# First chunk of a SiLU MLP kernel: eight groups on 384 transposed rows over narrow w1 slices, then on the last 128 rows in the same banks

## The chip, the cores and the metric

The kernel runs on one core of one Trainium2 chip. The metric is the device time of one execution in microseconds (us). Each run is marked as fast or slow (slow when over 1.5% above the fastest of its kernel); medians are over all runs of a set and given with the lowest and highest run.

PE is TensorE (matmuls), PEld its weight loads, ACT is ScalarE, DVE is VectorE, SP is SyncE. PE, ACT, DVE and SP each have a queue of instructions; DMAs are issued from SP and ACT here. "Landing" is the time at which all sixteen DMA engines have reported their share of a DMA. PSUM is the memory in which matmuls add up their results; the kernel uses eight banks of it, each of 128 x 512 fp32. A start flag marks the matmul that begins a new sum in a bank. The "grant" is the moment from which PE runs at its full clock. The chain that ended last is the row of waits and work that the profile follows back from the last instruction.

## The reference

A SiLU MLP, forward and backward, in bfloat16, with S = 2048 rows, D = 640, F = 1536:

```python
h   = x @ w1            # (S, F)
a   = silu(h)
out = a @ w2            # (S, D)
# and the gradients of x, w1, w2 for a given grad_out
```

The four outputs are `out`, `gx`, `gw1` and `gw2`.

## The kernel before

The rows are worked off in four chunks of 512. For a chunk, twelve groups (F = 12 x 128) of five matmuls (D = 5 x 128) make h transposed; ScalarE makes silu and tanh of it, VectorE the gradient factor. Then come `out` (the w2 phase) and the other gradients. From the w2 phase of the first chunk on, all operands are there in time, and PE works without a pause. The change is about what comes before: at the start nothing has been loaded, x must be transposed, and the first matmuls follow the DMAs.

The first chunk before: 256 rows of x are loaded and transposed on PE, the other 256 come through a DMA transpose, which landed 8.0 us after its issue. All twelve groups run first on the 256 PE-transposed rows, w1 slice by w1 slice (two groups share one PSUM bank), so that PE can start when the first of five slices is there (even its first half: slice 0 comes in two halves, one on each queue). Then all run on the other 256 rows.

```python
early += [load_x(nc.sync, 0), load_x(nc.scalar, 1)]
early += [load_w1(0, slice(0, F // 2)), load_w1(0, slice(F // 2, F), nc.scalar)]
early += [load_w1(k) for k in range(1, 3)]
for k in range(3, DT):
    load_w1(k)                                  # five slices of 128 x 1536, 393 KB each
nc.sync.dma_start_transpose(out=xT_next[:, :, HC:SC], in_=x2[HC:SC, :])     # HC = 256
...
def h_first(xT, aT, ghT):
    pe_x(xT)                                    # 10 transposes on PE, 3 copies
    halves = (slice(0, HC), slice(HC, SC))
    hs = [[ps_h.tile([P, 2, HC], FP32, name="hp") for _ in range(NPAIR)], []]
    for dt_ in range(DT):
        for pair in range(NPAIR):
            h_pair_mm(hs[0][pair], pair, dt_, xT, halves[0])        # 60 matmuls of 256 columns
    ...                                         # silu, four copies out of PSUM
    for pair in range(NPAIR):
        ...
        for q in range(2):
            for dt_ in range(DT):
                h_pair_mm(hp, pair, dt_, xT, halves[1], (q,))       # 60 more
        ...
```

Eighteen unneeded matmuls (`NWARM = 18`) run from the very start, before x is there, to bring PE to its fast clock.

Of the kernel before, what the change touches and what calls it, by code (L numbers as in the profile page):

```python
# [9 lines left out]
ACT = mybir.ActivationFunctionType  # L10
ALU = mybir.AluOpType
FP32 = mybir.dt.float32
# [3 lines left out]
def start_before_entry_wait(nc, names):  # L16




    def move(nc):
        blocks = nc.m.functions[0].blocks
        entry, home = blocks[0].instructions, blocks[1].instructions
        for engine in {i.engine for i in home if i.name in names}:
            mine = [i for i in home if i.engine == engine]
            last = max(k for k, i in enumerate(mine) if i.name in names)
            moved = mine[: last + 1]
            gate = next(
                k
                for k, i in enumerate(entry)  # L30
                if i.engine == engine and isinstance(i, mybir.InstEventSemaphore)
            )
            taken = {i.name for i in moved}
            for k in reversed(range(len(home))):
                if home[k].name in taken:
                    del home[k]
            for i in reversed(moved):
                entry.insert(gate, i)

    nc.at_finalize(move)  # L40
# [35 lines left out]
def kernel(  # L76
# [11 lines left out]
    nc = tc.nc  # L88
    P = 128
# [7 lines left out]
    F = w1.shape[1]  # L97
    ST, DT, FT = S // P, D // P, F // P
    SC = 512
# [4 lines left out]
    FB = FC // P  # L104
    LAG = 2
    NWARM = 18
    HC = 2 * P
    NPAIR = FT // 2
    NCOPY = 4
    dt_in = x.dtype  # L110

# [34 lines left out]
    with ExitStack() as mctx:  # L146
# [35 lines left out]
        def load_x(eng, q):  # L182
            return eng.dma_start(out=x_nat[:, q, :], in_=x_v[:, q, :])  # L183

        def load_w1(k, cols=slice(0, F), eng=nc.sync):
            return eng.dma_start(out=w1_nat[:, k, cols], in_=w1_v[:, k, cols])  # L186

        early += [load_x(nc.sync, 0), load_x(nc.scalar, 1)]
        early += [load_w1(0, slice(0, F // 2)), load_w1(0, slice(F // 2, F), nc.scalar)]
        early += [load_w1(k) for k in range(1, 3)]  # L190
        for k in range(3, DT):
            load_w1(k)
        nc.sync.dma_start_transpose(out=xT_next[:, :, HC:SC], in_=x2[HC:SC, :])
        start_before_entry_wait(nc, {i.ins.name for i in early})
        nc.scalar.activation(warm_a[:], warm[:, 0:1], ACT.Silu)
        nc.sync.dma_start(out=w2_nat[:], in_=w2_v[:])
# [4 lines left out]

        def pe_x(xT):
            slices = ((0, 1), (1, 3), (3, DT))
            tps = [ps_h.tile([P, hi - lo, 2, P], dt_in, name="tp", tag="hp") for lo, hi in slices]
            for q in range(2):
                for tp, (lo, hi) in zip(tps, slices):
                    for dt_ in range(lo, hi):
                        nc.tensor.transpose(
                            tp[:, dt_ - lo, q, :], x_nat[:, q, dt_ * P:(dt_ + 1) * P], ident[:]
                        )  # L210
            for k, (tp, (lo, hi)) in enumerate(zip(tps, slices)):
                copy_tp = nc.scalar.copy if k % 2 else nc.vector.tensor_copy
                copy_tp(out=xT[:, lo:hi, 0:HC], in_=tp[:].rearrange("p k q s -> p k (q s)"))

# [10 lines left out]
        def silu_a(ft, hp, aT):  # L225
            nc.scalar.activation(aT[:, ft, :], hp[:], ACT.Silu)  # L226
# [13 lines left out]
            silu_a(ft, hp, aT)  # L240
            silu_grad(ft, hp, aT, ghT)

        def h_pair_mm(hp, pair, dt_, xT, cols, qs=(0, 1)):
            for q in qs:
                ft = 2 * pair + q
                nc.tensor.matmul(  # L246
                    hp[:, q, :],
                    lhsT=w1_nat[:, dt_, ft * P:(ft + 1) * P],
                    rhs=xT[:, dt_, cols],
                    start=(dt_ == 0 and q == qs[0]),  # L250
                    stop=(dt_ == DT - 1 and q == qs[-1]),
                )

        def pair_silu(hp, pair, aT, cols):
            nc.scalar.activation(aT[:, 2 * pair:2 * pair + 2, cols], hp[:], ACT.Silu)

        def pair_grad(hp, pair, aT, ghT, cols):
            fts = slice(2 * pair, 2 * pair + 2)
            t = tpool.tile([P, 2, HC], FP32, name="t")
            nc.scalar.activation(t[:], hp[:], ACT.Tanh, scale=0.5)  # L260
            v = tpool.tile([P, 2, HC], dt_in, name="v")
            nc.vector.tensor_scalar(out=v[:], in0=t[:], scalar1=-0.5, scalar2=0.5, op0=ALU.mult, op1=ALU.add)
            nc.vector.scalar_tensor_tensor(
                out=ghT[:, fts, cols], in0=aT[:, fts, cols], scalar=1.0, in1=v[:],
                op0=ALU.subtract, op1=ALU.mult,
            )

        def h_first(xT, aT, ghT):
            pe_x(xT)
            halves = (slice(0, HC), slice(HC, SC))  # L270
            hs = [[ps_h.tile([P, 2, HC], FP32, name="hp") for _ in range(NPAIR)], []]
            for dt_ in range(DT):
                for pair in range(NPAIR):
                    h_pair_mm(hs[0][pair], pair, dt_, xT, halves[0])
            for pair in range(NPAIR):
                pair_silu(hs[0][pair], pair, aT, halves[0])
                if pair < NCOPY:
                    h_sb = hpool.tile([P, 2, HC], FP32, name="h_sb")
                    nc.vector.tensor_copy(out=h_sb[:], in_=hs[0][pair][:])
                    hs[0][pair] = h_sb  # L280
            grads = [(0, pair) for pair in list(range(NCOPY, NPAIR)) + list(range(NCOPY))]
            grads += [(1, pair) for pair in range(NPAIR)]
            for pair in range(NPAIR):
                hp = ps_h.tile([P, 2, HC], FP32, name="hp")
                hs[1].append(hp)
                for q in range(2):
                    for dt_ in range(DT):
                        h_pair_mm(hp, pair, dt_, xT, halves[1], (q,))
                pair_silu(hp, pair, aT, halves[1])
                if 1 <= pair <= 3:  # L290
                    half, done = grads.pop(0)
                    pair_grad(hs[half][done], done, aT, ghT, halves[half])
            for half, pair in grads:
                pair_grad(hs[half][pair], pair, aT, ghT, halves[half])

        def g_group(ft, goT, ghT):
            gp = ps_h.tile([P, SC], FP32, name="hp")
# [32 lines left out]
        for c in range(NCH):  # L330
            xT, goT = xT_next, goT_next
            aT = apool.tile([P, FT, SC], dt_in, name="aT")
            ghT = apool.tile([P, FT, SC], dt_in, name="ghT")

            if c + 1 < NCH:
                xT_next = load_xT(c + 1)
                goT_next = load_goT(c + 1)
            if c == 1:
                for j in range(0, ST, STC):
                    nc.sync.dma_start(out=go_nat[:, j:j + STC, :], in_=go_v[:, j:j + STC, :])  # L340
            if c == 2:
                for j in range(0, ST, STC):
                    rows = slice(max(j, 2), j + STC)
                    nc.sync.dma_start(out=x_nat[:, rows, :], in_=x_v[:, rows, :])

            if c == 0:
                h_first(xT, aT, ghT)
                nc.sync.dma_start(
                    out=aT_scr[:, c * SC:(c + 1) * SC].rearrange("(ft p) s -> p ft s", p=P), in_=aT[:]
                )  # L350
                sd_phase(c, w2_nat, aT, oT_scr)
                for ft in range(FT):
                    g_group(ft, goT, ghT)
                nc.sync.dma_start(
                    out=ghT_scr[:, c * SC:(c + 1) * SC].rearrange("(ft p) s -> p ft s", p=P), in_=ghT[:]
                )
                sd_phase(c, w1T, ghT, gxT_scr)
                continue

            for i in range(FT + LAG):  # L360
                if i < FT:
                    h_group(i, xT, aT, ghT)
                if i >= LAG:
                    g_group(i - LAG, goT, ghT)

            store_rows(c - 1, opool)
            nc.sync.dma_start(
                out=aT_scr[:, c * SC:(c + 1) * SC].rearrange("(ft p) s -> p ft s", p=P), in_=aT[:]
            )
            nc.sync.dma_start(  # L370
                out=ghT_scr[:, c * SC:(c + 1) * SC].rearrange("(ft p) s -> p ft s", p=P), in_=ghT[:]
            )
            if c == NCH - 1:
                load_a_blk(0, w1pool, "w1a")

            sd_phase(c, w2_nat, aT, oT_scr)
            sd_phase(c, w1T, ghT, gxT_scr)
# [121 lines left out]
```

## Time and profile before

| | before |
|---|---|
| time, first set | 320.62 us median of 3 (320.48 to 320.81) |
| span of the profiled execution | 318.8 us |
| PE busy | 313.6 us (98%) |
| PE's share of the chain that ended last | 96% |
| first w1 matmul / start of the w2 phase | 3.85 / 18.41 us |

The page's first part, busy time of each engine with its share of the span:

```profile
PE 313.6 (98%) x1516; PEld 150.5 (47%) x1544; DVE 102.8 (32%) x182; ACT 76.8 (24%) x139; POOL 0.7 (0%) x6
```

PE leaves almost nothing to win, except at the start. This is the chain that ended last, in order of time (start in us, duration in us, what):

```profile
1.47 6.41 DMA w_nat<-in_w_dram
7.88 0.05 issue
7.92 10.65 PE hp L246 x96
18.58 0.21 PE hp L315
```

The chain runs through a w1 slice until 7.88 us, then through 96 matmuls (L246) without a pause, then into the w2 phase (L315). The timeline of PE up to there has the start in us, the duration in us, engine, line, operation, shapes and count, and in brackets the idle time before, with what ended it:

```profile
0.50 2.10 PE L160 MATMUL wp<-warm 128*128 128x128 bf16 x18 [0.50 <-DVE warm L156]
2.64 1.25 PE L208 MATMUL tp<-ident,x_nat 128*128 128x128 bf16 x10
3.85 1.72 PE L246 MATMUL hp<-xT,w_nat 128*128 128x256 bf16 x12
5.79 1.48 PE L246 MATMUL hp<-xT,w_nat 128*128 128x256 bf16 x12 [0.22 <-DMA w_nat<-in_w_dram]
7.92 10.65 PE L246 MATMUL hp<-xT,w_nat 128*128 128x256 bf16 x96 [0.65 <-DMA w_nat<-in_w_dram]
18.41 13.11 PE L315 MATMUL hp<-aT,w_nat 128*128 128x512 bf16 x58
```

PE had to wait before its second and third row of twelve w1 matmuls. A bracket counts the wait from the modelled end of the matmul before; the starts of neighbouring matmuls are 0.38 and 0.82 us further apart than the usual 109 ns there, 1.20 us in all. The first row itself was a little slow: three of the spacings of its matmuls were 165 to 213 ns, 0.25 us too much.

### The profile page before, as it was taken

What the parts mean: (1) busy time and instruction counts of PE and PEld (TensorE: products, weight loads), DVE (VectorE), ACT (ScalarE), POOL (GpSimd) and SP (SyncE); (2) the same over time, 40 slices, a digit from 0 to 9 for tenths busy, and PEclk for the clock granted to TensorE, in tenths of its full rate; (3) what the DMA queues carried; (4) which work ended last, traced back from release to release, by engine and by line L of the source; (5) the groups of instructions that cost most, each with busy time, mean ns of one, the idle gap of its engine ahead of it and who ended that gap; (6) DMA issues with size and microseconds to landing.
All of it is one profiled execution on the core that took longest, in us unless ns stands there. A gap on an engine that the chain in (4) does not pass through costs nothing.

```text
span 318.8 us, 3632 instructions
## 1 busy us (share of the span) xinstructions
PE 313.6 (98%) x1516; PEld 150.5 (47%) x1544; DVE 102.8 (32%) x182; ACT 76.8 (24%) x139; POOL 0.7 (0%) x6
## 2 busy tenths in 40 slices
PE   8999999999999999999999999999999999999997
PEld 6854444444444444444444444444444444444444
DVE  1495641477410087710147741000000100001001
ACT  2691000545201354411054520110100001001010
POOL 0000000000000000000000000000000000000000
DMA  8999999999989986492635079909999999997111
GB/s 280 293 181 192 221 249 260 349 252 280 292 214 343 230 155 176 169 310 76 168 110 141 0 256 267 221 20 297 211 245 254 204 251 326 236 313 217 65 35 49
DMA packets 147233, 67.02 MB, mean 210 GB/s; under 512 B 113937, under 2 KB 146705, under 8 KB 147217
## 3 DMA queue, kind: packets, MB, share of 16 engines
q1 hardware_dynamic: 146928, 66.43, 83.3%
q10 hardware_dynamic: 288, 0.36, 0.3%
q8 instruction: 12, 0.20, 0.2%
q14 instruction: 5, 0.03, 0.0%
HBM read 9.18 MB, written 28.97 MB: 120 GB/s over the span
## 4 chain that ended last, share of the span: by engine, by line
PE 96%; DMA 2%; issue 1%; SPq 0%; DVE 0%; DVEq 0%
PE hp L315 32%; PE hp L299 16%; PE hp L404 16%; PE hp L455 15%; PE hp L217 12%; PE hp L246 3%; DMA w_nat<-in_w_dram 2%; PE hp L435 1%; SPq L186 0%; SPq L183 0%; DVE g L446 0%; DVEq L446 0%; SPq L483 0%
## 5 line engine op out<-in xcount | busy, mean ns | idle before, releaser
L299 PE MATMUL hp<-goT,w2T 128*128 128x512 bf16 x239 | 56.8, 379 | 0.1
L315 PE MATMUL hp<-ghT,w1T 128*128 128x512 bf16 x235 | 52.2, 379 | 0.3
L315 PE MATMUL hp<-aT,w_nat 128*128 128x512 bf16 x234 | 52.1, 379 | 0.3
L404 PE MATMUL hp<-a_blk,go_nat 128*128 128x512 bf16 x235 | 51.7, 379 | 0.3
L455 PE MATMUL hp<-gh_blk,x_nat 128*128 128x512 bf16 x219 | 48.2, 379 | 0.3
L217 PE MATMUL hp<-xT,w_nat 128*128 128x512 bf16 x174 | 43.4, 379 | 0.3
L323 ACT ACTIVATE oT<-hp 128x512 bf16<-128x512 f32 x24 | 14.5, 604 | 106.8 <-PE hp L315 106.8
L299 PEld LDWEIGHTS <-w2T 128*128 128x128 bf16 x240 | 23.5, 98 | 28.3
L404 PEld LDWEIGHTS <-go_nat 128*128 128x128 bf16 x240 | 23.5, 98 | 28.3
L315 PEld LDWEIGHTS <-w1T 128*128 128x128 bf16 x240 | 23.4, 98 | 28.4
L315 PEld LDWEIGHTS <-w_nat 128*128 128x128 bf16 x240 | 23.5, 98 | 28.1
L306 DVE SCALAR_TENSOR_TENSOR ghT<-ghT,hp 128x512 bf16<-128x512 bf16 x48 | 32.5, 683 | 7.3 <-PE hp L299 7.3
L455 PEld LDWEIGHTS <-x_nat 128*128 128x128 bf16 x224 | 21.9, 98 | 26.4
L325 DVE CAST oT<-hp 128x512 bf16<-128x512 f32 x16 | 11.1, 691 | 72.2 <-PE hp L315 67.7
L226 ACT ACTIVATE aT<-hp 128x512 bf16<-128x512 f32 x36 | 21.5, 597 | 30.4 <-PE hp L217 30.4
L217 PEld LDWEIGHTS <-w_nat 128*128 128x128 bf16 x180 | 17.6, 98 | 21.2
L233 DVE SCALAR_TENSOR_TENSOR ghT<-aT,v 128x512 bf16<-128x512 bf16 x36 | 24.7, 686 | 0.2
L232 DVE TENSOR_SCALAR v<-t 128x512 bf16<-128x512 f32 x36 | 15.4, 427 | 26.7 <-ACT t L230 26.7
L230 ACT ACTIVATE t<-hp 128x512 f32<-128x512 f32 x36 | 21.3, 591 | 0.0
L466 DVE CAST g<-hp 128x512 bf16<-128x512 f32 x7 | 4.8, 692 | 47.0 <-PE hp L455 27.0
L414 DVE CAST g2T<-hp 128x512 bf16<-128x512 f32 x7 | 4.8, 692 | 46.1 <-PE hp L404 46.1
L412 ACT ACTIVATE g2T<-hp 128x512 bf16<-128x512 f32 x8 | 4.8, 597 | 47.0 <-PE hp L404 47.0
(28 smaller groups left out, 76.4 us busy)
## 6 DMA issues: line engine op xcount, KB each, us to landing
aT_scr<-aT SPq DMA_DIRECT2D x4, 1536.0 KB, 6.3
ghT_scr<-ghT SPq DMA_DIRECT2D x4, 1536.0 KB, 8.2
out_dram<-o_sb SPq DMA_DIRECT2D x8, 640.0 KB, 3.3
oT_scr<-oT SPq DMA_DIRECT2D x4, 640.0 KB, 3.6
go_nat<-in_grad_out_dram SPq DMA_DIRECT2D x4, 640.0 KB, 8.1
gxT_scr<-oT SPq DMA_DIRECT2D x4, 640.0 KB, 4.8
w_nat<-in_w_dram SPq DMA_DIRECT2D x1, 1920.0 KB, 11.0
x_nat<-in_x_dram SPq DMA_DIRECT2D x3, 640.0 KB, 7.4
```

Source lines behind the costliest of these rows:

```text
L217: nc.tensor.matmul(hp[:], lhsT=w1_nat[:, dt_, ft * P:(ft + 1) * P], rhs=xT[:, dt_, :], start=(dt_ == 0), stop=(dt_ == DT - 1),)
L226: nc.scalar.activation(aT[:, ft, :], hp[:], ACT.Silu)
L230: nc.scalar.activation(t[:], hp[:], ACT.Tanh, scale=0.5)
L232: nc.vector.tensor_scalar(out=v[:], in0=t[:], scalar1=-0.5, scalar2=0.5, op0=ALU.mult, op1=ALU.add)
L233: nc.vector.scalar_tensor_tensor(out=ghT[:, ft, :], in0=aT[:, ft, :], scalar=1.0, in1=v[:], op0=ALU.subtract, op1=ALU.mult)
L299: nc.tensor.matmul(gp[:], lhsT=w2T[:, dt_, ft * P:(ft + 1) * P], rhs=goT[:, dt_, :], start=(dt_ == 0), stop=(dt_ == DT - 1),)
L306: nc.vector.scalar_tensor_tensor(out=ghT[:, ft, :], in0=ghT[:, ft, :], scalar=1.0, in1=gp[:], op0=ALU.add, op1=ALU.mult)
L315: nc.tensor.matmul(op_[:], lhsT=w_all[:, ft, dt_ * P:(dt_ + 1) * P], rhs=rhs_all[:, ft, :], start=(ft == 0), stop=(ft == FT - 1),)
L323: nc.scalar.activation(oT[:, dt_, :], op_[:], ACT.Copy)
L325: nc.vector.tensor_copy(out=oT[:, dt_, :], in_=op_[:])
L404: nc.tensor.matmul(gp[:], lhsT=go_nat[:, st, dt_ * P:(dt_ + 1) * P], rhs=a_blk[:, st, :], start=(st == 0), stop=(st == ST - 1),)
L455: nc.tensor.matmul(gp[:], lhsT=x_nat[:, st, dt_ * P:(dt_ + 1) * P], rhs=gh_blk[:, st, :], start=(st == 0), stop=(st == ST - 1),)
```

## The change

Its intent: the first part shall need fewer bytes of w1. Eight groups, one per bank, run on 384 PE-transposed rows over slices of 1024 columns (262 KB). The DMA transpose brings only 128 rows. When they are there, the same eight groups take them into the same banks (128 more columns of the bank, without a start flag), and the last four groups run on all 512 rows at once, with the last 512 columns of w1.

```diff
-    HC = 2 * P
-    NPAIR = FT // 2
+    NQ = 3
+    HC = NQ * P
+    NA = 8
+    FA = NA * P
...
-        early += [load_x(nc.sync, 0), load_x(nc.scalar, 1)]
-        early += [load_w1(0, slice(0, F // 2)), load_w1(0, slice(F // 2, F), nc.scalar)]
-        early += [load_w1(k) for k in range(1, 3)]
+        early += [load_x(nc.sync, 0), load_x(nc.scalar, 1), load_x(nc.sync, 2)]
+        early += [load_w1(0, slice(0, FA), nc.scalar)]
+        early += [load_w1(k, slice(0, FA)) for k in range(1, 3)]
         for k in range(3, DT):
-            load_w1(k)
+            load_w1(k, slice(0, FA))
         nc.sync.dma_start_transpose(out=xT_next[:, :, HC:SC], in_=x2[HC:SC, :])
+        nc.sync.dma_start(out=w1_nat[:, :, FA:F], in_=w1_v[:, :, FA:F])
...
-            for q in range(2):
+            for q in range(NQ):
...
+            for dt_ in range(DT):
+                for ft in range(NA):
+                    mm(ft, dt_, slice(0, HC), dt_ == 0, False)
+            for ft in range(NA):
+                for dt_ in range(DT):
+                    mm(ft, dt_, slice(HC, SC), False, dt_ == DT - 1)
+                silu_a(ft, hs[ft], aT)
+                if ft < NCOPY:
+                    h_sb = hpool.tile([P, SC], FP32, name="h_sb")
+                    nc.vector.tensor_copy(out=h_sb[:], in_=hs[ft][:])
+                    hs[ft] = h_sb
+            grads = list(range(NCOPY, NA))
+            for ft in range(NA, FT):
+                hs.append(ps_h.tile([P, SC], FP32, name="hp"))
+                h_mm(hs[ft], ft, xT)
+                silu_grad(grads[0], hs[grads[0]], aT, ghT)
+                grads.pop(0)
+                silu_a(ft, hs[ft], aT)
+            for ft in list(range(NA, FT)) + list(range(NCOPY)):
+                silu_grad(ft, hs[ft], aT, ghT)
```

More of the change, by code (lines that the diff above doesn't have):

```diff
@@ L203, in pe_x @@
             slices = ((0, 1), (1, 3), (3, DT))
-            tps = [ps_h.tile([P, hi - lo, 2, P], dt_in, name="tp", tag="hp") for lo, hi in slices]
-            for q in range(2):
+            tps = [ps_h.tile([P, hi - lo, NQ, P], dt_in, name="tp", tag="hp") for lo, hi in slices]
+            for q in range(NQ):
                 for tp, (lo, hi) in zip(tps, slices):
@@ L241, in h_group, with h_first, mm @@
             silu_grad(ft, hp, aT, ghT)
-        def h_pair_mm(hp, pair, dt_, xT, cols, qs=(0, 1)):
-            for q in qs:
-                ft = 2 * pair + q
+        def h_first(xT, aT, ghT):
+            pe_x(xT)
+            hs = [ps_h.tile([P, SC], FP32, name="hp") for _ in range(NA)]
+            def mm(ft, dt_, cols, start, stop):
                 nc.tensor.matmul(
-                    hp[:, q, :],
+                    hs[ft][:, cols],
                     lhsT=w1_nat[:, dt_, ft * P:(ft + 1) * P],
@@ L249, in h_pair_mm @@
                     rhs=xT[:, dt_, cols],
-                    start=(dt_ == 0 and q == qs[0]),
-                    stop=(dt_ == DT - 1 and q == qs[-1]),
-                )
-        def pair_silu(hp, pair, aT, cols):
-            nc.scalar.activation(aT[:, 2 * pair:2 * pair + 2, cols], hp[:], ACT.Silu)
-        def pair_grad(hp, pair, aT, ghT, cols):
-            fts = slice(2 * pair, 2 * pair + 2)
-            t = tpool.tile([P, 2, HC], FP32, name="t")
-            nc.scalar.activation(t[:], hp[:], ACT.Tanh, scale=0.5)
-            v = tpool.tile([P, 2, HC], dt_in, name="v")
-            nc.vector.tensor_scalar(out=v[:], in0=t[:], scalar1=-0.5, scalar2=0.5, op0=ALU.mult, op1=ALU.add)
-            nc.vector.scalar_tensor_tensor(
-                out=ghT[:, fts, cols], in0=aT[:, fts, cols], scalar=1.0, in1=v[:],
-                op0=ALU.subtract, op1=ALU.mult,
-            )
@@ L268, in h_first @@
-        def h_first(xT, aT, ghT):
-            pe_x(xT)
-            halves = (slice(0, HC), slice(HC, SC))
-            hs = [[ps_h.tile([P, 2, HC], FP32, name="hp") for _ in range(NPAIR)], []]
-            for dt_ in range(DT):
-                for pair in range(NPAIR):
-                    h_pair_mm(hs[0][pair], pair, dt_, xT, halves[0])
-            for pair in range(NPAIR):
-                pair_silu(hs[0][pair], pair, aT, halves[0])
-                if pair < NCOPY:
-                    h_sb = hpool.tile([P, 2, HC], FP32, name="h_sb")
-                    nc.vector.tensor_copy(out=h_sb[:], in_=hs[0][pair][:])
-                    hs[0][pair] = h_sb
-            grads = [(0, pair) for pair in list(range(NCOPY, NPAIR)) + list(range(NCOPY))]
-            grads += [(1, pair) for pair in range(NPAIR)]
-            for pair in range(NPAIR):
-                hp = ps_h.tile([P, 2, HC], FP32, name="hp")
-                hs[1].append(hp)
-                for q in range(2):
-                    for dt_ in range(DT):
-                        h_pair_mm(hp, pair, dt_, xT, halves[1], (q,))
-                pair_silu(hp, pair, aT, halves[1])
-                if 1 <= pair <= 3:
-                    half, done = grads.pop(0)
-                    pair_grad(hs[half][done], done, aT, ghT, halves[half])
-            for half, pair in grads:
-                pair_grad(hs[half][pair], pair, aT, ghT, halves[half])
@@ new lines, in mm @@
+                    start=start,
+                    stop=stop,
+                )
+            for dt_ in range(DT):
+                for ft in range(NA):
[8 more added lines that the diff above has]
+                    hs[ft] = h_sb
@@ L342 @@
                 for j in range(0, ST, STC):
-                    rows = slice(max(j, 2), j + STC)
+                    rows = slice(max(j, NQ), j + STC)
                     nc.sync.dma_start(out=x_nat[:, rows, :], in_=x_v[:, rows, :])
```

## The prediction

> **What bounds the kernel now.** TensorE (PE): busy 313.6 of 318.8 us (98%), 96% of the chain of waits that ended last. The change touches only the first 18 us, so it can win only what PE loses there. In the timeline the x transposes start at 2.64 us, the first w1 matmul (128x256) at 3.85, and PE stands before w1 slices until 5.79 (0.22 us idle) and 7.92 (0.65 us); the chain runs through that w1 load (1.47 to 7.88 us). From 7.92 the remaining 96 matmuls run unbroken at 109 ns each to 18.41, where the w2 phase begins. 3.85 plus 120 x 109 ns would be 16.9: about 1.5 us are lost, 0.25 to slow first matmuls (12 at about 131 ns), 1.2 to late w1.
>
> **What the change does, costed.**
> - Matmul time hardly changes. Spacings read from the trace: 512 columns 216 ns (five in 1.08 us), 256 columns 109; the kernel's last group (16 of 384 and 16 of 128 columns, 3.66 us) gives 162 and about 55. Before 120 x 109 = 13.1 us; after 40 x 162 + 40 x 55 + 20 x 216 = 13.0. The Trainium skill ("TensorE: Matmul & The Clock Gate", Back-to-back issue gap) has about 81 ns for 128 columns with weight loads; this trace decides, else +1 us.
> - Five more transposes (ten took 1.25 us) on a third x slice, and copies of 384 columns: the first w1 matmul moves from 3.85 to about 4.4 (+0.5).
> - x and w1 bytes before the first part can finish: 2.29 MB before, 1.80 after. PE still needs 1.3 us per w1 slice, but a slice is 262 KB, not 393. From arrivals before (4.1, 5.75, 7.88, about 8.7 and 9.8) I estimate 4.4, 5.3, 6.9, 7.9, 8.8. Then no slice costs PE more than about 0.2 us; the first part ends near 11.0, the twelve groups near 17.5 to 17.7.
> - New limit: w2 landed at 17.9 (issued 6.94, 11.0 to landing), 0.5 us before its use. The bytes ahead of it are the same; I expect 17.5 to 17.8, so it may take part back.
> - ScalarE/VectorE: eight silus from about 11.5 at about 0.5 us pitch, then alternating with four tanh; the last silu ends near 19.4, before its use at about 20.4. The gradient chain on VectorE ends about 1 us later (28), before its first use at 31.5. Banks come free in time.
> - One start flag per bank, then a second column range without it, is sound by the Trainium skill ("PSUM — Partial Sum Buffer", The four PSUM rules: the flag clears the whole bank's written bits).
>
> **On the critical path:** +0.5 (later start), -1.0 to -1.2 (w1 waits), -0.1 (matmul sum, slow matmuls), 0 to +0.2 (w2): net about -0.7 us. The other 300 us are untouched. Predicted 319.9 us, 8-in-10 range 319.3 to 320.9. Chances: faster by over 2% 0.01, within 2% 0.98, slower 0.01.
>
> **What would show it.** First w1 matmul at about 4.4; PE idle before w1 under 0.3 us; 128-column matmuls spaced 55 ns; the w2 phase at about 17.7, perhaps with idle put down to the w2 load; no new PE wait after; PE busy about the same.
>
> **What would make it wrong.** Slices arriving no earlier, because a slow DMA engine rather than bytes sets their landing (320.7 to 321.1); w2 late; 128-column matmuls at 80 ns; more slow matmuls; waits moved by the changed order of DMA semaphores.

## The result, and the profile after

| | before | after |
|---|---|---|
| time, median of 6 | 320.52 us (320.27 to 320.81) | 319.88 us (319.59 to 320.81) |
| ratio of fast runs | | 0.9984, 95% interval 0.9969 to 0.9999 |
| profiled execution | 320.54 us, span 318.8 | 320.81 us, span 319.0 |

A ratio is the mean time of one kernel's fast runs over that of the other's of the same rounds, so it isn't quite the ratio of the medians. The median fell by 0.64 us, to within 0.02 us of the prediction. But the execution that was profiled is the slowest of the six, slower than the one profiled before. The number came out right; the profile says something else than the prediction's sum.

The page's first part, after:

```profile
PE 314.5 (99%) x1501; PEld 147.7 (46%) x1529; DVE 102.9 (32%) x182; ACT 77.2 (24%) x139; POOL 0.7 (0%) x6
```

The chain that ended last, in order of time, after:

```profile
0.54 3.51 DMA x_nat<-in_x_dram
4.05 0.05 issue
4.10 0.71 PE tp L211 x5
4.81 0.02 issue
4.83 9.71 PE hp L251 x80
14.54 0.21 PE hp L220
...
18.86 6.69 PE hp L299 x31
```

The w1 load is gone from the chain. In its place stands the third x slice, which landed at 4.05 us, and from 4.83 us on nothing but PE. The timeline of PE, after (same columns as before):

```profile
0.51 2.10 PE L162 MATMUL wp<-warm 128*128 128x128 bf16 x18 [0.51 <-DVE warm L158]
2.56 1.25 PE L211 MATMUL tp<-ident,x_nat 128*128 128x128 bf16 x10
4.10 0.71 PE L211 MATMUL tp<-ident,x_nat 128*128 128x128 bf16 x5 [0.29 <-DMA x_nat<-in_x_dram]
4.83 9.71 PE L251 MATMUL hp<-xT,w_nat 128*128 128x384 bf16 x80
14.38 4.48 PE L220 MATMUL hp<-xT,w_nat 128*128 128x512 bf16 x19
18.70 13.11 PE L299 MATMUL hp<-aT,w_nat 128*128 128x512 bf16 x59
```

PE starts on w1 at 4.83 instead of 3.85 us and then has no pause; the w2 phase starts at 18.70 instead of 18.41. Where did the gain go? The timeline of the weight loads, which come one per matmul, shows it (after):

```profile
5.10 0.15 PEld L251 LDWEIGHTS <-w_nat 128*128 128x128 bf16 x1 [0.17 <-issue]
5.42 0.15 PEld L251 LDWEIGHTS <-w_nat 128*128 128x128 bf16 x1 [0.17 <-issue]
5.74 0.15 PEld L251 LDWEIGHTS <-w_nat 128*128 128x128 bf16 x1 [0.17 <-issue]
6.06 0.15 PEld L251 LDWEIGHTS <-w_nat 128*128 128x128 bf16 x1 [0.17 <-issue]
6.38 7.98 PEld L251 LDWEIGHTS <-w_nat 128*128 128x128 bf16 x74 [0.17 <-issue]
```

Until 6.4 us the loads, and so the matmuls of 384 columns, are 320 ns apart, then 162: PE ran on half its clock. The trace has a record of the full clock's being granted at 6.53 us after the first instruction. (The profile's column for the granted clock shows 1.00 from the start: it knows of no clock before its first record. One has to read the spacing.) The Trainium skill ("TensorE: Matmul & The Clock Gate", Part 1) describes this: PE's clock is halved until PE has been busy through a window of about 3.4 us, and these windows run freely, so that where the kernel's start falls in one is chance. In the execution profiled before, the full speed came at about 4.4 us.

From this, four numbers make up the start of the w2 phase: the first w1 matmul; the matmuls at full speed (13.1 us before, and 40 x 162.5 + 40 x 56 + 20 x 216 ns = 13.06 us after); half of the time spent at half the clock; and waits. Before: 3.85 + 13.1 + 0.25 + 1.20 = 18.40 (trace: 18.41). After: 4.83 + 13.06 + (6.53 - 4.83)/2 = 18.74 (trace: 18.70).

### The profile page after: what moved, and what is told of

Its sections match the earlier page's. It is cut to its first block, busy times and chain, and to the rows that moved or that the text cites. A ratio compares the mean times of both kernels' runs of the same rounds, so it can differ in the third digit from the quotient of the medians.

```text
span 319.0 us, 3604 instructions
## 1 busy us (share of the span) xinstructions
PE 314.5 (99%) x1501; PEld 147.7 (46%) x1529; DVE 102.9 (32%) x182; ACT 77.2 (24%) x139; POOL 0.7 (0%) x6
## 4 chain that ended last, share of the span: by engine, by line
PE 98%; DMA 1%; issue 1%; SPq 0%; DVE 0%; DVEq 0%
PE hp L299 32%; PE hp L283 16%; PE hp L388 16%; PE hp L439 15%; PE hp L220 13%; PE hp L251 3%; DMA x_nat<-in_x_dram 1%; PE hp L419 1%; PE tp L211 0%; SPq L185 0%; DVE g L430 0%; DVEq L430 0%; SPq L467 0%
## 5 line engine op out<-in xcount | busy, mean ns | idle before, releaser
L220 PE MATMUL hp<-xT,w_nat 128*128 128x512 bf16 x192 | 47.8, 379 | 0.4
L229 ACT ACTIVATE aT<-hp 128x512 bf16<-128x512 f32 x48 | 28.5, 614 | 37.6 <-PE hp L220 30.4
L299 PEld LDWEIGHTS <-w_nat 128*128 128x128 bf16 x240 | 23.5, 98 | 28.3
L236 DVE SCALAR_TENSOR_TENSOR ghT<-aT,v 128x512 bf16<-128x512 bf16 x48 | 32.6, 685 | 0.3
L220 PEld LDWEIGHTS <-w_nat 128*128 128x128 bf16 x200 | 19.6, 98 | 23.3
L235 DVE TENSOR_SCALAR v<-t 128x512 bf16<-128x512 f32 x48 | 20.0, 425 | 28.2 <-ACT t L233 28.2
L233 ACT ACTIVATE t<-hp 128x512 f32<-128x512 f32 x44 | 26.5, 620 | 0.0
```

What stands on the lines that cost most here:

```text
L220: nc.tensor.matmul(hp[:], lhsT=w1_nat[:, dt_, ft * P:(ft + 1) * P], rhs=xT[:, dt_, :], start=(dt_ == 0), stop=(dt_ == DT - 1),)
L229: nc.scalar.activation(aT[:, ft, :], hp[:], ACT.Silu)
L233: nc.scalar.activation(t[:], hp[:], ACT.Tanh, scale=0.5)
L235: nc.vector.tensor_scalar(out=v[:], in0=t[:], scalar1=-0.5, scalar2=0.5, op0=ALU.mult, op1=ALU.add)
L236: nc.vector.scalar_tensor_tensor(out=ghT[:, ft, :], in0=aT[:, ft, :], scalar=1.0, in1=v[:], op0=ALU.subtract, op1=ALU.mult)
L299: nc.tensor.matmul(op_[:], lhsT=w_all[:, ft, dt_ * P:(dt_ + 1) * P], rhs=rhs_all[:, ft, :], start=(ft == 0), stop=(ft == FT - 1),)
```

## The experiments

Twelve runs, in three sets of four (e1 to e4, e5 to e8, e9 to e12), each set on one chip, with the kernel before timed beside them. The changed kernel was timed in the first and the third of these sets, not in the second, so e6, e7 and e8 can be compared with it only across chips. Three times the changed kernel or the kernel before was run unedited, because one trace of such a start turned out to be one draw. All results were correct. The table has each trace's four terms; "sum" is the first w1 matmul + matmuls at full speed + half of the slow time + waits after that start. Grants are the trace's clock records, or, where it has none, read from the spacing of the matmuls.

| trace | first w1 matmul | full clock at | slow cost | waits | sum | w2 phase starts | time of this run |
|---|---|---|---|---|---|---|---|
| before | 3.85 | 4.4 | 0.25 | 1.20 | 18.40 | 18.41 | 320.54 |
| e5, before again | 3.79 | 6.18 | 1.1 | 0.3 | 18.3 | 18.31 | 320.46 |
| after | 4.83 | 6.53 | 0.85 | 0 | 18.74 | 18.70 | 320.81 |
| e1, after again | 4.47 | 5.94 | 0.73 | 0 | 18.26 | 18.23 | 320.34 |
| e12, after again | 4.72 | 3.88 | 0 | 0 | 17.78 | 17.78 | 319.89 |
| e2 | 5.46 | 3.28 | 0 | 0 | 18.52 | 18.52 | 320.63 |
| e3 | 4.23 | 5.04 | 0.40 | 0 | 17.69 | 17.66 | 319.76 |
| e4 | 7.01 | 4.44, lost 7.86 to 11.27 | 1.70 | 0 | 21.77 | 21.75 | 323.88 |
| e6 | 5.03 | 8.64 | 1.80 | 0 | 19.89 | 19.85 | 321.96 |
| e7 | 5.11 | before 5.1 | 0 | 0 | 18.17 | 18.17 | 320.33 |
| e8 | 4.80 | 8.28 | 1.74 | 0 | 19.60 | 19.54 | 321.73 |
| e9 | 5.03 | 4.82 | 0 | 0 | 18.09 | 18.09 | 320.22 |
| e10 | 5.02 | 6.13 | 0.56 | 0 | 18.64 | 18.60 | 320.71 |
| e11 | 6.10 | 3.97 | 0 | 0 | 19.16 | 19.16 | 321.30 |

In all fourteen the sum is right to within 0.06 us, and the time of the run less the start of the w2 phase is 302.1 to 302.2 us. So nothing after the start of the w2 phase differs in these traces. The sum is bookkeeping, not a test of causes: it says how much each term took in a trace. If the rest is as constant in runs that have no trace, their w2 phase started at their time less 302.1 us.

### e1: the changed kernel again

No edit. Expected:

> The changed kernel once more, unedited, to see how far it scatters (319.6 to 320.8 us in six runs, before 320.3 to 320.8) and to get a second trace. Theory C (slow first matmuls decide the scatter): in the first trace six 384-column matmuls from 4.83 us on were spaced 320 ns instead of 162, about 0.95 us lost, and that execution was the slowest of the six (320.81). A faster execution must show fewer of them: about two at 319.8 us, the w2 phase near 18.0 instead of 18.86 us. Rival D (the DMA decides): the number of slow matmuls stays near six in a faster execution too, and what moved is the landing of the third x slice (4.05 us in the first trace) or of w1.

Measured: 320.34 us in the profiled run, median 320.56 (320.34 to 323.85); before in the same rounds 320.84 (320.54 to 322.2). The trace's chain has the w1 matmuls here:

```profile
4.47 9.60 PE hp L251 x80
```

The grant came at 5.94 us; five of the 384-column matmuls were slow (the last one in part), not six. The third x slice landed at 3.48 instead of 4.05 us, so that the transposes had no pause and the first w1 matmul came 0.36 us earlier. Both theories have a part, but not an equal one: of the 0.47 us by which this run was faster, the earlier start has 0.36 and the slow clock 0.12 (0.73 against 0.85). Theory C's "about two" slow matmuls belonged to 319.8 us, a time that this trace didn't reach. Two of the six runs (322.56 and 323.85) are 2 us and more above the rest and make the ratio to before 1.0013, though the median is 0.28 us lower. Those two have no trace.

### e2: PE's pauses filled

```diff
+            def fill(n, q): ...
             for q in range(NQ):
+                if q == NQ - 1:
+                    fill(4, q - 1)       # matmuls of x rows with the identity into an unused bank
...
+            fill(3, NQ - 1)
             for k, (tp, (lo, hi)) in enumerate(zip(tps, slices)):
```

> Seven unneeded ordinary matmuls (128 columns, about 105 ns each) on loaded x rows fill PE's two pauses: four between the second and third x slice (3.8 to 4.1 us) and three between the transposes and the first w1 matmul. They wait for no other data than the transposes around them. Theory C: PE's activity is then unbroken, the fast clock comes earlier and at a steadier time, at most three slow 384-column matmuls, mean 0.3 to 0.6 us below the changed kernel and its scatter under 0.5 us. Rival D: slow matmuls as many as before, time the same or up to 0.3 us longer, by the part of the filling that delays the transposes of the third slice.

Measured: median 320.76 us (320.24 to 321.18), ratio 0.9993. No 384-column matmul was slow, as theory C has it, but that proves nothing about the filling: the grant came at 3.28 us, and the first added matmul ran at 3.39. The median didn't fall by 0.3 to 0.6 us, and the scatter was 0.94 us, not under 0.5. In the profiled run the first w1 slice landed only at 5.41 us:

```profile
5.46 8.91 PE L260 MATMUL hp<-xT,w_nat 128*128 128x384 bf16 x80 [0.84 <-DMA w_nat<-in_w_dram]
```

This line is also the matmul sum at full speed: 80 matmuls in 8.91 us, 40 of them at 162.5 ns and 40 at 56 (with the last one's 0.17 us of latency).

### e3 and e6: the first w1 slice behind the third x slice

```diff
-        early += [load_w1(0, slice(0, FA), nc.scalar)]
+        early += [load_w1(0, slice(0, FA))]
```

> The first w1 slice goes out on the same queue as the third x slice, behind it, instead of on ScalarE's queue beside it. If the third slice lands late (4.05 us, 3.5 after its issue) because the first w1 slice shares the DMA engines with it: it lands near 3.4, the transposes run without the 0.3 us pause, the first w1 matmul starts near 4.5 instead of 4.83, if w1 is there, and the time is 0.3 us shorter. If the start is set by w1 landing (4.5 us in the trace) as much as by x: the start stays near 4.8 and the time within 0.1 us.

> The kernel of e3 (first w1 slice behind the third x slice on one queue), unedited, to tell its gain from scatter. If all slices on one queue help by landing in the order of use, w1 matmuls start at 4.2 to 4.5 us and the median is again 0.4 to 0.8 us below before, measured in the same rounds. If e3 was luck: as the changed kernel, within 0.3 us of before.

Measured in e3: the third x slice landed at 3.17 us, the first w1 slice at 4.13, the first w1 matmul ran at 4.23, and the median was 320.12 us (319.69 to 321.83) against 320.56 of e1 in the same rounds; the ratio to before was 0.9982 (0.9960 to 1.0004). In e3's trace the w1 matmuls had the earliest start of the changed kernel and its variants:

```profile
4.23 9.28 PE L251 MATMUL hp<-xT,w_nat 128*128 128x384 bf16 x80
```

That the w1 slice beside it holds up the third x slice isn't shown. In e1 and e12, with the w1 slice beside it, the third x slice landed at 3.48 and 3.42 us; in e6, the kernel of e3 again, at 3.45. In e6, on another chip, the same kernel took 320.04 and 320.30 us in two runs, and 321.96 to 322.20 in four. The profiled run is one of the four:

```profile
5.03 10.67 PE L251 MATMUL hp<-xT,w_nat 128*128 128x384 bf16 x80 [0.57 <-DMA w_nat<-in_w_dram]
```

Here the w1 slice landed at 4.99 us, and PE stood still from the last transpose to 5.03. The start is 0.8 us later than in e3, but the time is 2.2 us longer, because the slow clock cost 1.80 us instead of 0.40: the grant came at 8.64 us, one window of 3.41 us after 5.23. In the timeline of weight loads the spacing is still 0.32 us at 8.2 us and single from 8.5 on (e6):

```profile
7.89 0.15 PEld L251 LDWEIGHTS <-w_nat 128*128 128x128 bf16 x1 [0.17 <-issue]
8.21 0.15 PEld L251 LDWEIGHTS <-w_nat 128*128 128x128 bf16 x1 [0.17 <-issue]
8.53 4.55 PEld L251 LDWEIGHTS <-w_nat 128*128 128x128 bf16 x28 [0.17 <-issue]
```

By the count at e8, PE was at work for 0.70 of the window that ended at 5.23; by estimate a PE without the pause of 0.8 us would have reached about 0.9. So the pause probably cost itself and a missed window, which is up to 3.41/2 = 1.7 us. No edit shows this. The order of e3 is no safe gain: it was 0.9982 of before on one chip and 1.0031 of before (1.0008 to 1.0054) on another.

### e4: full w1 slices

```diff
-        early += [load_w1(0, slice(0, FA), nc.scalar)]
-        early += [load_w1(k, slice(0, FA)) for k in range(1, 3)]
+        early += [load_w1(0, slice(0, F), nc.scalar)]
+        early += [load_w1(k) for k in range(1, 3)]
         for k in range(3, DT):
-            load_w1(k, slice(0, FA))
+            load_w1(k)
-        nc.sync.dma_start(out=w1_nat[:, :, FA:F], in_=w1_v[:, :, FA:F])
```

> Undoes the narrow w1 slices alone: each of the five slices is loaded over all 1536 columns again (393 KB), nothing else changed; the later load of the last four groups' columns goes. My theory B (bytes ahead of a slice set its landing): slices again land near 5.9, 8.0, 9 and 10 us, PE needs the third by about 8 (start 4.83, two rows of 1.3 us, slow matmuls), so waits on w1 of 0.2 to 1.0 us come back and the time rises by that. Rival S (late landings come from one slow DMA engine, whatever the bytes): the landings and the time are as with narrow slices, within 0.1 us.

Measured: three runs of 320.12 to 321.04 us and three of 323.56 to 325.02 (the last is marked slow); the ratio of the fast runs is 1.0014, as good as e1's 1.0013, though the median, 322.3 (slow run included), is 1.7 us above e1's. The profiled run is a late one, and not for the reason that theory B gives: the slice it waited for is the first, which landed at 6.96 us. The trace's sixteen increments of that DMA's semaphore came at

```text
3.92 3.96 3.97 4.00 4.07 4.08 4.09 4.11 4.12 4.16 4.22 4.23 4.37 4.86 5.08 6.96
```

Fifteen engines had their share there by 5.08 us, and the sixteenth took 1.9 us more. The Trainium skill ("DMA: Bandwidth & Descriptors", Why a DMA increments its semaphore by 16 and not by 1) says that the engines finish independently and that only the full count means "landed"; here is what this can cost. PE stood still for 2.6 us, and then lost its clock. The windows of e4, from the span's start in us (busy time and count of each engine, granted clock, DMA share, GB/s):

```profile
core 0: us, PE busy (x) PEld busy (x) DVE busy (x) ACT busy (x) POOL busy (x), PEclk, DMA share, GB/s
6.00:7.00 1.00, 0.00 (x0) 0.00 (x0) 0.00 (x0) 0.00 (x0) 0.00 (x0) 1.00 0.94 353
7.00:8.00 1.00, 0.99 (x6) 0.63 (x7) 0.00 (x0) 0.00 (x0) 0.00 (x0) 0.93 1.03 399
8.00:9.00 1.00, 1.00 (x5) 0.46 (x3) 0.00 (x0) 0.00 (x0) 0.00 (x0) 0.50 1.63 274
9.00:10.00 1.00, 1.00 (x4) 0.46 (x3) 0.00 (x0) 0.00 (x0) 0.00 (x0) 0.50 0.68 134
10.00:11.00 1.00, 1.00 (x4) 0.46 (x3) 0.00 (x0) 0.00 (x0) 0.00 (x0) 0.50 1.09 311
11.00:12.00 1.00, 1.00 (x7) 0.59 (x6) 0.00 (x0) 0.00 (x0) 0.00 (x0) 0.86 1.07 364
```

Granted at 4.44 us, lost at 7.86, granted again at 11.27: exactly 3.41 us apart, the windows of which the skill speaks. Later slices made PE wait nowhere in this trace. The landings themselves speak for B: the third, fourth and fifth slice came at 7.95, 8.90 and 9.85 us, near the 8.0, 9 and 10 of the expectation. In the three traces with full slices (before, e5, e4) the third landed at 7.41 to 7.95 and the fifth at 9.32 to 9.85; in the eleven with narrow slices at 5.97 to 7.21 and 7.37 to 8.54. So S is wrong about the landings. What the earlier landings save in time isn't settled: the expected waits on the third slice couldn't be seen behind a first slice that late (by estimate, e12's start at 4.72 us with rows of 1.3 us needs the third slice at 7.32 and would have waited 0.1 to 0.6 us for a full one), and the best runs of e4 and e1 (320.12 and 320.34 us) don't differ in B's favour.

### e5: the kernel before again

No edit.

> The kernel before, unedited, for a second trace. In the first, the last DMA engine's share of the second and third w1 slice came 0.9 to 1.5 us after the median engine's, beside one 3,072-byte packet that took 2,046 ns where the others took 121. Theory R (such a late packet is chance, another one in each execution): this trace has other late packets, and the wait for w1 after the first w1 matmul differs from 0.87 us, anywhere from 0 to 2 us. Rival S (one engine is always slow): the same two slices are the late ones, waits near 0.9 us again. In both, the start of the w2 phase is the start of the first w1 matmul (about 3.9) + 13.1 us + half of the time run on the slow clock + waits, within 0.2 us, and what follows takes 300.2 us as in all six traces so far.

Measured: median 320.69 us (320.46 to 321.12); before in the same rounds 320.59 (319.73 to 321.75). The first w1 matmul, and the chain behind the second slice:

```profile
3.79 14.69 PE L246 MATMUL hp<-xT,w_nat 128*128 128x256 bf16 x120
```

```profile
0.99 5.47 DMA w_nat<-in_w_dram
6.46 0.05 issue
6.51 11.96 PE hp L246 x108
```

Theory R holds: now the second slice was the late one (6.46 instead of 5.74 us), the third was in time. And the grant came at 6.18, so that the first twelve matmuls ran at 213 ns. Yet the w2 phase began at 18.31 us, as good as before (18.41). At full speed the first row would have been over at 3.79 + 12 x 0.109 = 5.1 us, and PE would have waited for the second slice until 6.46. The slow clock was hidden behind the DMA: slow clock and waits together cost 1.45 us in the first trace and 1.4 us here. This may be why the runs of before scattered so little in the first set (320.27 to 320.81): what the clock takes, the wait for w1 gives back. It isn't the whole story, for in the other sets the runs of before scattered by 1.7, 2.0 and 0.9 us.

### e7: two x slices

```diff
-    NQ = 3
+    NQ = 2
-        early += [load_x(nc.sync, 0), load_x(nc.scalar, 1), load_x(nc.sync, 2)]
+        early += [load_x(nc.sync, 0), load_x(nc.scalar, 1)]
```

> Undoes the third x slice alone: 256 PE-transposed rows, narrow w1 slices and eight groups stay, the other 256 rows come by the DMA transpose. Mine: w1 matmuls start near 3.9 us again, but eight groups on 256 rows need only 0.87 us per w1 slice, less than a slice takes to land, and the first part is over by about 8.5 to 9 us, before the DMA transpose of 256 rows has landed (11.1 us before, about 9.6 to 10.2 with fewer bytes ahead). PE waits 1 to 1.5 us there; w2 phase at 19.0 to 19.5, time 0.4 to 1.0 us above the changed kernel. Rival (the third slice only costs, the gain is all in the narrow slices): the w2 phase comes 0.5 us earlier than the changed kernel's, time 0.5 us below it.

Measured: 320.33 to 324.42 us, median 321.98, ratio 1.0049 (1.0015 to 1.0084). Neither expectation was met, as far as can be told: both were relative to the changed kernel, which wasn't timed in this set. In the trace (the fastest run) the first w1 matmul waited for the first w1 slice until 5.11 us, and after it PE had no pause:

```profile
5.11 8.91 PE L251 MATMUL hp<-xT,w_nat 128*128 128x256 bf16 x80 [1.47 <-DMA w_nat<-in_w_dram]
```

The DMA transpose of 256 rows, which I had expected at 9.6 to 10.2, landed at 8.99, 0.5 us before its use at 9.5. The idle time in front of the first w1 matmul is what remains, and it is longer with ten transposes (from 3.5 us on) than with fifteen. What the five slower runs lost I can't show; they have no trace.

### e8: one warm-up matmul

```diff
-    NWARM = 18
+    NWARM = 1
```

> One warm-up matmul instead of eighteen: PE is idle until the x transposes at about 2.5 us. Theory C (the fast clock is granted at the end of the first window of about 3.4 us in which PE was nearly always at work, the windows lying anywhere to the start; so between about 3.2 and 6.6 us with PE at work from 0.5 us; seen 3.28, 5.04, 5.94 and 6.53): the grant now comes between 5.3 and 8.7 us, slow matmuls cost half of the time from 4.5 us to there, 0.4 to 2.1 us, so the mean is about 0.9 us above the changed kernel. Rival F (the grant comes a fixed time after the kernel's start, whatever PE does): grant before 6.6 us as with eighteen, time unchanged within 0.3 us.

Measured: median 321.52 us (320.84 to 323.91), 0.9 us above before in the same rounds (320.59), ratio 1.0052 (1.0021 to 1.0084). How far it lies above the changed kernel can't be said. The grant came at 8.28 us, inside the range of theory C and outside that of F. That the missing matmuls made the grant late isn't shown by this one trace: e6, with all eighteen and on the same chip, had it at 8.64 us. The timeline has the idle time at the start and the slow first part, 80 matmuls in 10.59 us instead of 8.91:

```profile
0.51 0.29 PE L162 MATMUL wp<-warm 128*128 128x128 bf16 x1 [0.51 <-DVE warm L158]
2.58 1.25 PE L211 MATMUL tp<-ident,x_nat 128*128 128x128 bf16 x10 [1.78 <-DMA x_nat<-in_x_dram]
4.06 0.71 PE L211 MATMUL tp<-ident,x_nat 128*128 128x128 bf16 x5 [0.23 <-DMA x_nat<-in_x_dram]
4.80 10.59 PE L251 MATMUL hp<-xT,w_nat 128*128 128x384 bf16 x80
```

With these traces the windows can be counted: go back from each grant in steps of 3.41 us, and add up the columns that PE worked on in each window. The windows that ended in a grant had PE at work for 0.78 to 0.97 of the time (before 0.90, after 0.81, e10 0.78, e2 0.82; e6 and e8 in full), the last ones without a grant for 0.49 to 0.73 (e8 0.49, e1 0.56, e5 0.62, e6 0.70, after 0.73). So the limit lies near three quarters in this count, if the windows have the same length in every trace (only e4 shows two in a row). It hangs on counting columns: by the profile's busy time, which counts overlapping latencies too, the granted window of e2 and the refused one of e6 both have 2.77 of 3.41 us, 0.81. And it only works if transposes count as work: without them the granted windows go down to 0.34 (e10) and the refused ones up to 0.56 (after), and nothing separates them.

### e9, e10, e11, e12: two repairs, and the changed kernel beside them

e9 has both, e10 the first alone, e11 the second alone, e12 is unedited.

```diff
-        early += [load_w1(0, slice(0, FA), nc.scalar)]
+        early += [load_w1(0, slice(0, FA // 2)), load_w1(0, slice(FA // 2, FA), nc.scalar)]   # e9, e10
...
+            fill(5, NQ - 1)       # e9, e11: five unneeded matmuls behind the last transpose
             for k, (tp, (lo, hi)) in enumerate(zip(tps, slices)):
```

> The changed kernel with two repairs: the first w1 slice in two halves of 512 columns, one on each queue, so that the first four groups can start on the first half; and five unneeded matmuls on x between the last transpose and the first w1 matmul, so that PE has no pause there. Theory W (the fast clock is granted at the end of a window of 3.41 us in which PE worked for about 80% or more; a pause before the first w1 matmul makes it miss a window, 1.7 us lost): first w1 matmul at 4.4 to 4.8 us, no pause over 0.3 us, grant never later than 6.7 us, all six runs within 1.2 us of each other and none 1.5 us above the fastest; w2 phase at 17.6 to 18.6, median 0.4 to 0.9 us below before. Rival D (late DMA packets make the slow runs): runs 1.5 us or more above the fastest remain, about one in four.

> The split first w1 slice alone, without the added matmuls. Theory W: most runs as e9 or 0.1 to 0.2 us faster, but one or two of six 1.7 us slower where the first half lands late. Rival D: as e9.

> The five added matmuls alone, the first w1 slice whole on ScalarE's queue as in the changed kernel. Theory W: the pause before the first w1 matmul shrinks by about 0.5 us, so runs 1.7 us above the fastest become rarer than in the changed kernel of the same rounds (at most one of six), but the start still waits for the whole slice (4.4 to 5.4 us). Rival D: as the changed kernel of the same rounds.

> The changed kernel once more, on the same chip and in the same rounds as the three repairs. Theory W: of six runs, those near 319.6 to 320.8 us have the grant by 6.7 us, and one to three are 1.7 us slower (a missed window); median within 0.7 us of before. Rival D: runs spread evenly, no step near 1.7 us.

| | median | lowest to highest | ratio to before |
|---|---|---|---|
| before | 320.36 | 319.98 to 320.90 (11 runs) | |
| e12, changed | 320.04 | 319.56 to 320.46 (5) | 0.9991 (0.9979 to 1.0003) |
| e9, split and filled | 320.17 | 320.06 to 320.41 (5) | 0.9995 (0.9982 to 1.0008) |
| e10, split | 320.26 | 320.11 to 320.71 (5) | 1.0001 (0.9989 to 1.0013) |
| e11, filled | 321.01 | 320.30 to 322.78 (6) | 1.0025 (1.0006 to 1.0045) |

The repairs miss their aim: no version beats the changed kernel. e9 has the small scatter that I expected (0.35 us), but its median is 0.19 us below before, not 0.4 to 0.9. Its first half slice landed at 4.99 us in the profiled run, with fourteen of the sixteen engines done by 4.06: the smaller DMA, too, was held up by late engines. e11 was to have fewer slow runs than e12 and had one where e12 had none; its profiled run waited for w1 until 6.05 us. And e12 had none of the "one to three" slow runs that I expected on this chip, and e10 none of its "one or two"; with three of the four versions free of slow runs, the set can't tell theory W from rival D. What the traces say of a single execution stands; how often a run misses a window, on which chip, I can't predict. e12's trace is the changed kernel at its best:

```profile
2.63 1.59 PE L211 MATMUL tp<-ident,x_nat 128*128 128x128 bf16 x15
4.72 8.91 PE L251 MATMUL hp<-xT,w_nat 128*128 128x384 bf16 x80 [0.49 <-DMA w_nat<-in_w_dram]
13.46 4.48 PE L220 MATMUL hp<-xT,w_nat 128*128 128x512 bf16 x20
17.78 13.11 PE L299 MATMUL hp<-aT,w_nat 128*128 128x512 bf16 x60
```

The grant at 3.88 us came during the transposes, no matmul on w1 was slow, and the w2 phase started 0.6 us earlier than in the first trace of before.

## Why the prediction was right or wrong

The time (319.9 predicted, 319.88 measured) and the class were right. That they agree to 0.02 us is luck. In the three sets in which both kernels were timed, the medians differ by 0.64, 0.28 and 0.32 us in favour of the change; the predicted 0.7 lies above them all. The means of the fast runs, from which the ratios are made, differ by -0.5, +0.4 and -0.3 us, and only the first set's interval (0.9969 to 0.9999) leaves out 1. Term by term:

- **"The change touches only the first 18 us": right.** The time less the start of the w2 phase is 302.1 to 302.2 us in all traces. No new wait came later. VectorE's gradient chain ended at 29.0 us in the trace of after (28 predicted), and its first result was used at 32.9.
- **Matmul sum, -0.1 us: right.** 13.06 against 13.1 us; matmuls of 128 columns were 56 ns apart (predicted "about 55"), not the 81 ns of the skill.
- **Later start, +0.5 us: too small.** The first w1 matmul came at 4.83, 4.47 and 4.72 us in the three traces of the changed kernel, against 3.85 and 3.79 before: +0.85 in the mean. I had counted transposes and copies, but two DMAs set it: the third x slice (landing at 4.05 in the first trace, with fifteen of sixteen engines done by 3.67) and the first w1 slice, now one DMA of 262 KB on ACT's queue (4.47, 4.35, 4.67). Before, PE could start on the first half of that slice, 197 KB, which landed at 3.60 and 3.42.
- **w1 waits, -1.0 to -1.2 us: right about the changed kernel, taken from one draw for before.** After the start, PE waited for w1 in none of the three traces; the slices landed at 4.47, 4.99, 6.56, 7.22 and 7.85 us in the first, mostly earlier than the 4.4 to 8.8 that I had estimated. The 1.2 us before was one draw: in e5 it was 0.3, with the slow clock taking 1.1 in its place. In the first trace of before one packet of 3,072 bytes took 2,046 ns where the median took 121 (two more took about 1,030), and the last engines' shares of the third and fourth slice came about 1.5 us after the middle ones; that the packet made these late isn't shown, since the trace doesn't name a packet's engine. I had named a slow DMA engine as a risk to the change; it was as much an accident in my baseline.
- **Slow first matmuls, part of "-0.1": wrong.** The slow clock cost 0.85, 0.73 and 0 us in the changed kernel, and 0.25 and 1.1 before. I took it for a constant. It is a draw, and the change alters what a bad draw costs: before, a slow first row is hidden behind the wait for w1 (e5); after, there is no such wait, and every slow matmul lengthens the time. That fits the wider scatter of the first set (319.59 to 320.81 against 320.27 to 320.81), but in e12's set the two scatter alike (0.90 and 0.92 us).
- **w2, 0 to +0.2 us: not needed.** w2 landed at 16.6 us in the first trace, 17.0 in e12 and 17.5 in e1, each time before the w2 phase; I had expected 17.5 to 17.8. The DMA transpose of 128 rows instead of 256 landed at 8.6 rather than 11.1 us, and w2 was issued at 4.90 rather than 6.94.

With the measured terms the prediction's sum reads, for the mean of three traces against two: +0.85 for the start, -0.75 for the waits (1.20 and 0.3 before), -0.15 for the slow clock (0.53 against 0.68), -0.04 for the matmuls: about -0.1 us. Waits and slow clock together gave 0.9 us (1.43 before, 0.53 after), where the prediction had 1.0 to 1.2 from the waits alone, and the later start took nearly all of it back. The medians of six, six and five runs are the better measure of the time and say -0.3 to -0.6. So the prediction had the direction, and the size in the first set; of its steps the start was mis-sized by 0.35 us, and the slow clock, which the change lays open, stood in the sum as a constant ("more slow matmuls" was named among the risks alone).

The start flag did what the prediction took for sound: with one flag per bank, all results of e1 to e4 and e6 to e12 were correct.

What stays open: how much time the narrow slices by themselves save (e4 shows that they land earlier, not what this is worth); what makes some packets take more than ten times as long; and how often a run misses a clock window, since most slow runs have no trace.

## What to carry to other kernels

At the start of a kernel, one trace is one draw: a late DMA engine and the phase of the clock windows each moved about a microsecond or more here, so read the start from two or three executions before counting a wait as something to win. When two delays run side by side, taking away one wins only what the other doesn't cover, and puts the other on the path. A pause of PE in the first few microseconds can cost more than itself, because the window it spoils is followed by one at half the clock: in e4 the pause of 2.6 us cost 1.70 us more. Filling such pauses with unneeded matmuls (e2, e9, e11) showed no gain here.

## What the Trainium skill lacked or had wrong

- "TensorE: Matmul & The Clock Gate", Part 1, has the free-running windows of about 3.4 us, and the runs agree (3.41 us between grant, loss and grant in e4). It doesn't say how busy PE must be in one: here, counted by columns, windows with PE at work for 0.78 or more of the time were granted the full clock, those with 0.73 or less were not.
- The same page, Part 4, says that PE transposes don't count as busy for the clock in the way matmuls do. Here they seem to (the trace lists them as MATMUL and doesn't show in what mode they ran): in e12 the grant came at 3.88 us after a window in which ordinary matmuls filled 0.56 and transposes most of the rest, while in the trace of after a window with the same 0.56 of ordinary matmuls and fewer transposes was refused.
- The same page, Back-to-back issue gap, has about 81 ns for a stream of 128-column matmuls with weight loads; here they were 56 ns apart, and 512-column ones 216 ns (the page: about 131 in a stream). The formula that the section gives for an isolated matmul, N / 2.4 + 2.5 ns, fits both.
- "DMA: Bandwidth & Descriptors", Why a DMA increments its semaphore by 16 and not by 1, says that the engines finish independently, but not by how much: in e4 fifteen engines were done by 5.08 us and the last at 6.96, and in the first trace of before one packet of 3,072 bytes took 2,046 ns instead of 121.
